# Float32r matmuls over 384 tokens instead of 288, in attention followed by two feed-forward layers

## The chip, the core and the metric

The kernel runs on one core of a Trainium2 chip. The metric is the device time of one launch in microseconds. The five engines of the core have queues of their own: TensorE multiplies (PE in the profile; its weight loads stand apart as PEld), VectorE (DVE), ScalarE (ACT) and GpSimd (POOL) work on elements, SyncE (SP) issues DMAs. In this kernel TensorE reads both operands from SBUF and accumulates in tiles of PSUM, in banks of 512 Float32 values per partition; VectorE and ScalarE empty them.

## The reference

Three steps follow one another, all in Float32 on the host side (B = 4, H = 8, S = 576, D = 64; 2304 tokens of 512 features between the steps):

```
a = softmax(causal(q k^T / 8));  local = a v
mem_out = (phi(q) M_prev) / (phi(q) z_prev + 1e-6)
x = sigmoid(beta) mem_out + (1 - sigmoid(beta)) local        # to 2304 x 512
x = (silu(x w_gate) * (x w_val)) w_out                       # d_ff 1536
y = (h * sigmoid(1.702 h)) w_out2,  h = x w_in               # d_ff 2048
```

## The kernel before, in words

**Numbers in two parts.** The two layers multiply in Float32r, one pass of the array per matmul. To keep accuracy each operand is split in a high and a low part, and each product is the sum of three: high by high, high by low, low by high. In `proj` (L618) these are `(0, xh), (0, xl), (1, xh)`, where 0 and 1 choose the weights' high or low part.

**Two passes over the tokens.** The first pass (`moe`, L616) does both layers for two of the four batches, 1152 tokens; the second (`second`, L784) does the other two. Weights are decoded and split once, during the first pass, in an order of 68 blocks of 128 x 512 (`next_w`, `ahead`, L187 to L196), and written to DRAM for the second, which reads them ready or half ready (`next_block`, `ready`, L746 to L759), eight blocks ahead.

**First pass.** For each group g (3 in the first layer, 4 in the second) four hidden blocks of 128 features are made and then multiplied back to 4 blocks of 128 outputs (d). The 1152 tokens are taken in two halves of 576. A half has a PSUM tile of two banks, [128, 2, 512], and each of the 12 products of a block is issued as two matmuls of 288 columns, one per bank, with a weight load each:

```
for s in range(2):
    mm(t[:, s, :NS], wp[:, w, c:c + 128], x[:, kd, h, s * NS:(s + 1) * NS],
       kd == 0 and i == 0, kd == 3 and i == 2)
```

So a half of a block is 24 matmuls, with TensorE passing through `mm` (L82). ScalarE and VectorE then empty the tile: tanh and one multiply-add for a gate (L642, L643), one multiply for a value (L652), and `split_h` (L609) makes the two parts `hh` and `hl` of the hidden value. `back` (L599) multiplies four hidden blocks with one block of output weights, again 24 matmuls per half, and the result is added to `acc` (L663, L665, L694, L696) or, at the end, goes to `ot` and out (L699 to L708). PSUM is shared in two pools: `ps_m` with two tiles for this and `ps_s` with two for the attention.

**Attention beside it.** The attention of the first two batches runs alone at the start, up to some 120 us. That of the other two is cut into steps, with estimated costs, and these steps are put between the yields of `moe` in proportion: each yield gives `HALF`, the time planned for half of the 24 matmuls, and steps are taken as long as their costs are below the share that `MOE_T` allows. Under these steps the tile framework plans the order of each engine's queue by a timeline of its own (`schedule_with_timeline_sim`); on the chip each queue runs in that order.

**Second pass.** The products of x with the layer's input weights use Strassen's seven block products (`unit`, L807; `prod`, L793), with 288 columns in two banks each, and the weights `wb`. The second products of each group call `back` for two halves of 576 as the first pass does (L873 to L898). All PSUM tiles here come from `big` in turn from `ps_s` and `ps_m`. The very last half is cut into two pieces of 288. `blocks_of_x` (L955) reads the second pass's x back and forms the seven blocks of X while the first pass ends.

Of the kernel before, what the change touches and what calls it, by code (L numbers as in the profile page):

```python
# [8 lines left out]
F32 = mybir.dt.float32  # L9
# [26 lines left out]
def tile_attention_moe_moe(  # L36
# [57 lines left out]
    HALF = 1.475  # L94
# [514 lines left out]
    def split_h(t):  # L609
        hh = hpool.tile([128, 2, NS], F32R, tag="hh", name="hh")  # L610
        hl = hpool.tile([128, 2, NS], F32R, tag="hl", name="hl")
        nc.scalar.copy(hh, t)  # L612
        nc.vector.tensor_sub(hl, t, f(hh))  # L613
        return hh, hl

    def moe(xh, xl):  # L616

        def proj(wp, t, h):  # L618
            for kd in range(4):
                c = kd * 128  # L620
                for i, (w, x) in enumerate(((0, xh), (0, xl), (1, xh))):
                    for s in range(2):
                        mm(t[:, s, :NS], wp[:, w, c:c + 128], x[:, kd, h, s * NS:(s + 1) * NS],
                           kd == 0 and i == 0, kd == 3 and i == 2)
                if kd == 1:
                    yield HALF

        def big():
            t = ps_m.tile([128, 2, 512], F32, tag="m", name="m")
            return t, t[:, :, :NS]  # L630

        acc = x1.tile([128, 4, 2, 2, NS], F32, tag="acc", name="acc")
        for g in range(3):
            hs = []
            for i in range(4):
                wp = next_w()
                us = []
                for h in range(2):
                    t, tg = big()
                    yield from proj(wp, t, h)  # L640
                    u = up.tile([128, 2, NS], F32, tag="u", name="u")
                    nc.scalar.activation(u, tg, AF.Tanh, scale=0.5)  # L642
                    nc.vector.scalar_tensor_tensor(u, u, 1.0, tg, op0=ALU.add, op1=ALU.mult)  # L643
                    us.append(u)
                    yield HALF
                wp = next_w()
                hs.append([])
                for h in range(2):
                    u = us[h]
                    t, tv = big()  # L650
                    yield from proj(wp, t, h)
                    nc.vector.scalar_tensor_tensor(u, u, 0.5, tv, op0=ALU.mult, op1=ALU.mult)  # L652
                    hs[i].append(split_h(u))
                    yield HALF
                flush()
            for d in range(4):
                wp = next_w()
                for h in range(2):
                    o, t = big()
                    yield from back(hs, wp, o, h)  # L660
                    ac = acc[:, d, h]
                    if g == 0:
                        nc.scalar.copy(ac, t)  # L663
                    else:
                        nc.vector.tensor_add(ac, ac, t)  # L665
                    if g == 2:
                        yh = xh[:, d, h].rearrange("p (s n) -> p s n", s=2)
                        yl = xl[:, d, h].rearrange("p (s n) -> p s n", s=2)
# [3 lines left out]
        acc = x1.tile([128, 4, 2, 2, NS], F32, tag="acc", name="acc2")  # L672
        for g in range(4):
            hs = []
            for i in range(4):
                wp = next_w()
                hs.append([])
                for h in range(2):
                    t, th = big()
                    yield from proj(wp, t, h)  # L680
                    u = up.tile([128, 2, NS], F32, tag="u", name="u")
                    nc.scalar.activation(u, th, AF.Tanh, scale=0.851)
                    nc.vector.scalar_tensor_tensor(u, u, 1.0, th, op0=ALU.add, op1=ALU.mult)  # L683
                    hs[i].append(split_h(u))
                    yield HALF
            for d in range(4):
                wp = next_w()
                for h in range(2):
                    t0 = h * S
                    o, t = big()  # L690
                    yield from back(hs, wp, o, h)
                    ac = acc[:, d, h]
                    if g == 0:
                        nc.scalar.activation(ac, t, AF.Copy, scale=0.5)  # L694
                    elif g < 3:
                        nc.vector.scalar_tensor_tensor(ac, t, 0.5, ac, op0=ALU.mult, op1=ALU.add)  # L696
                    else:
                        ot = up.tile([128, 2, NS], F32, tag="u", name="ot")
                        nc.vector.scalar_tensor_tensor(ot, t, 0.5, ac, op0=ALU.mult, op1=ALU.add)  # L699

                        def store(d=d, ot=ot, t0=t0):
                            nc.sync.dma_start(
                                out=out[d * 128:(d + 1) * 128, t0:t0 + S],
                                in_=ot.rearrange("p s n -> p (s n)"),
                            )
# [4 lines left out]

# [73 lines left out]
    def second(X):  # L784
        turn = [0]

        def big():
            turn[0] += 1
            if turn[0] % 2:
                return ps_s.tile([128, 2, 512], F32, tag="s", name="m")  # L790
            return ps_m.tile([128, 2, 512], F32, tag="m", name="m")
# [48 lines left out]
        def split(t, scale, eng):  # L840
            hh = hpool.tile([128, 2, NS], F32R, tag="hh", name="hh")
            hl = hpool.tile([128, 2, NS], F32R, tag="hl", name="hl")
# [5 lines left out]
            return hh, hl  # L848

        for layer, n in enumerate((3, 4)):  # L850
            acc = x1.tile([128, 4, 2, 2, NS], F32, tag="acc", name="acc")
            for g in range(n):
                hs = [[None, None] for k in range(4)]
                if layer == 0:
                    for k in range(4):
                        gates = {}

                        def done(row, h, c):
                            if row == 0:
                                gates[h] = gate(c, 0.5)  # L860
                            else:
                                nc.gpsimd.tensor_mul(c, c, gates[h])
                                hs[k][h] = split(c, 0.5, nc.vector)

                        unit(done)
                else:
                    for k in (0, 2):

                        def done(row, h, c):
                            hs[k + row][h] = split(gate(c, 0.851), 1.0, nc.gpsimd if row else nc.vector)  # L870

                        unit(done)
                for d in range(4):  # L873
                    wp = next_block()
                    for h in range(2):
                        tail = layer == 1 and g == n - 1 and d == 3 and h == 1
                        for sub in ((0,), (1,)) if tail else ((0, 1),):
                            o = big()
                            for _ in back(hs, wp, o, h, sub):
                                pass  # L880
                            ac = acc[:, d, h, sub[0]:sub[-1] + 1]
                            t = o[:, sub[0]:sub[-1] + 1, :NS]
                            if layer == 0:
                                if g == 0:
                                    nc.scalar.copy(ac, t)
                                else:
                                    nc.vector.tensor_add(ac, ac, t)
                            elif g == 0:
                                nc.scalar.activation(ac, t, AF.Copy, scale=0.5)
                            elif g < n - 1:  # L890
                                nc.vector.scalar_tensor_tensor(ac, t, 0.5, ac, op0=ALU.mult, op1=ALU.add)
                            else:
                                ot = cu.tile([128, len(sub), NS], F32, tag="sn", name="ot")
                                nc.vector.scalar_tensor_tensor(ot, t, 0.5, ac, op0=ALU.mult, op1=ALU.add)
                                c0 = (2 + h) * S + sub[0] * NS
                                nc.sync.dma_start(
                                    out=out[d * 128:(d + 1) * 128, c0:c0 + len(sub) * NS],
                                    in_=ot.rearrange("p s n -> p (s n)"))  # L898
            if layer == 0:
                halves(lambda k, h: acc[:, k, h].rearrange("p s n -> p (s n)"), X)  # L900

    MOE_T = NCK * 4 * HALF
# [85 lines left out]
    flush()  # L988
    second(X)
# [42 lines left out]
```

## Time and profile before

| | |
|---|---|
| median of 3 runs | 1081.12 us (1080.79 to 1081.13) |
| span of the profiled execution | 1080.3 us |
| lying around the span, against the median | 0.8 us |
| TensorE matmul, weight load busy | 1041.8 us (96%), 971.8 us (90%) |
| VectorE, ScalarE, GpSimd busy | 696.1 us (64%), 542.9 us (50%), 612.3 us (57%) |
| TensorE matmuls in the trace | 7664 |
| DMA | 133.93 MB, mean 124 GB/s |

The profiler notes the start and the end of each instruction. Matmuls are pipelined: one is noted as busy until its result is in PSUM, so a busy TensorE can still be slower than it might be, and the distance from start to start is read where rows merge several matmuls ("x4"). The granted clock (PEclk) is TensorE's share of 2.4 GHz; 0.50 is 1.2 GHz.

### The profile page before, as it was taken

The numbers are of one execution on the slowest core, as the hardware profiler recorded it, in microseconds if no ns is written. First come the engines' busy times: TensorE is split into PE (matmuls) and PEld (weight loads), VectorE is DVE, ScalarE is ACT, GpSimd is POOL, SyncE is SP. The second block draws the span as 40 slices with busy tenths as digits, with TensorE's granted clock in tenths as the row PEclk, the third lists the DMA queues.
The fourth block names the chain that finished last, engine by engine and source line by source line (L and its number), as shares of the span: only waits on it lengthen the run. The fifth ranks groups of instructions, "written<-read, shape, count | busy, mean of one in ns | idle before, by whom it ended". The sixth has DMA issues, their size and how long they took to land.

```text
span 1080.3 us, 19843 instructions
## 1 busy us (share of the span) xinstructions
PE 1041.8 (96%) x7664; PEld 971.8 (90%) x7664; DVE 696.1 (64%) x1063; ACT 542.9 (50%) x1107; POOL 612.3 (57%) x634
## 2 busy tenths in 40 slices
PE   5989798999999999999999999999999999999998
PEld 2656687899999898989899999999999999999998
DVE  6887589646666777836657448762745778265573
ACT  4887555655545555756556454442513436343230
POOL 6886798866567475665745542661835817153321
PEclk8999999999999999999999999999999999999999
DMA  4332635644454453444434337323222222322102
GB/s 165 114 95 87 216 118 187 219 148 146 151 170 142 132 174 123 157 137 147 161 122 140 115 127 278 110 71 110 70 79 87 85 78 70 112 74 74 59 21 88
DMA packets 46718, 133.93 MB, mean 124 GB/s; under 512 B 7584, under 2 KB 10400, under 8 KB 46624
## 3 DMA queue, kind: packets, MB, share of 16 engines
q1 hardware_dynamic: 46480, 132.67, 36.7%
q8 instruction: 60, 0.98, 0.4%
q14 instruction: 34, 0.28, 0.1%
q10 hardware_dynamic: 144, 0.00, 0.0%
HBM read 92.54 MB, written 40.11 MB: 123 GB/s over the span
## 4 chain that ended last, share of the span: by engine, by line
PE 54%; DVE 3%; ACT 1%; DMA 1%; POOL 1%; issue 1%; SPq 0%; ACTq 0%; DVEq 0%; POOLq 0%
PE m L82 51%; PE o L82 1%; PE s L82 1%; DVE hl L613 1%; PE tp L378 1%; DMA xr<-x 0%; DMA raw<-w 0%; DVE u L683 0%; ACT hh L612 0%; ACT wb L742 0%; POOL wa L150 0%; DVE xl L766 0%; DMA x<-st 0%; DVE wa L147 0%; POOL p L366 0%
## 5 line engine op out<-in xcount | busy, mean ns | idle before, releaser
L82 PE MATMUL m<-hh,wp 128*128 128x288 f32 x1792 | 312.6, 297 | 1.4 <-ACT acc L663 0.7
L82 PEld LDWEIGHTS m<-hh,wp 128*128 128x128 f32 x1792 | 262.2, 189 | 9.5 <-issue 3.2
L82 PE MATMUL m<-xh,wp 128*128 128x288 f32 x1280 | 241.8, 304 | 12.6 <-DVE u L643 8.9
L743 POOL TENSOR_TENSOR wb<-raw,wb 128x256 fp32r<-128x256 f32 x140 | 124.9, 906 | 197.4 <-ACT wb L742 192.3
L82 PEld LDWEIGHTS m<-xh,wp 128*128 128x128 f32 x1280 | 193.9, 191 | 23.8 <-DVE u L643 8.1
L82 PE MATMUL m<-hl,wp 128*128 128x288 f32 x896 | 190.6, 296 | 0.0
L150 POOL TENSOR_TENSOR wa<-wa,wr 128x512 uint32<-128x512 uint32 x68 | 93.6, 1377 | 106.3 <-issue 50.2
L82 PEld LDWEIGHTS m<-hl,wp 128*128 128x128 f32 x896 | 143.6, 188 | 0.4 <-issue 0.4
L82 PE MATMUL m<-xl,wp 128*128 128x288 f32 x640 | 138.2, 298 | 0.0
L82 PE MATMUL m<-xh,wb 128*128 128x288 f32 x640 | 119.0, 296 | 0.0
L169 POOL TENSOR_TENSOR wp<-wa,wp 128x512 fp32r<-128x512 f32 x68 | 92.7, 1364 | 42.5 <-ACT wp L166 42.1
L82 PEld LDWEIGHTS m<-xl,wp 128*128 128x128 f32 x640 | 104.4, 191 | 0.0
L82 PEld LDWEIGHTS m<-xh,wb 128*128 128x128 f32 x640 | 96.9, 189 | 0.0
L742 ACT CAST wb<-raw 128x256 fp32r<-128x256 f32 x140 | 55.6, 404 | 79.1 <-PE m L82 77.6
L366 POOL TENSOR_SCALAR p<-p,sm 128x128 f32<-128x128 f32 (+3 forms) x128 | 75.1, 605 | 28.6 <-DVE sm L357 8.5
L82 PE MATMUL m<-th,wb 128*128 128x288 f32 x480 | 90.3, 296 | 0.0
L144 DVE TENSOR_SCALAR wa<-wa 128x512 f32<-128x512 f32 x68 | 39.3, 578 | 75.6 <-ACT wa L140 75.0
L341 ACT ACTIVATE p<-s,nm 128x128 f32<-128x128 f32 (+3 forms) x128 | 66.0, 528 | 30.5 <-DVE nm L327 29.3
L82 PEld LDWEIGHTS m<-th,wb 128*128 128x128 f32 x480 | 73.2, 189 | 0.0
L140 ACT ACTIVATE wa<-w 128x512 f32<-128x512 f32 x68 | 46.0, 677 | 53.5 <-POOL wp L169 48.9
L613 DVE TENSOR_TENSOR hl<-u,hh 128x576 fp32r<-128x576 f32 x56 | 56.4, 1007 | 25.4 <-ACT hh L612 24.6
L141 ACT ACTIVATE wr<-w 128x512 uint32<-128x512 uint16 x68 | 46.1, 678 | 51.0 <-POOL wa L150 50.4
(136 smaller groups left out, 1830.6 us busy)
## 6 DMA issues: line engine op xcount, KB each, us to landing
w<-w SPq DMA_DIRECT2D x40, 512.0 KB, 3.7
raw<-w SPq DMA_DIRECT2D x20, 896.0 KB, 4.6
w<-wo SPq DMA_DIRECT2D x28, 512.0 KB, 3.6
w<-wp SPq DMA_DIRECT2D x28, 512.0 KB, 2.9
wp<-w SPq DMA_DIRECT2D x28, 512.0 KB, 3.5
w<-sums SPq DMA_DIRECT2D x20, 512.0 KB, 2.8
qk<-qk SPq DMA_DIRECT2D x32, 288.0 KB, 3.7
nq<-nat SPq DMA_DIRECT2D x16, 320.0 KB, 4.1
```

The lines of the kernel that those rows point to most:

```text
L82: nc.tensor.matmul(o, w, x, start=start, stop=stop)
L140: nc.scalar.activation(a, top.bitcast(F32), AF.Abs)
L141: nc.scalar.activation(r, rest, AF.Copy, scale=2.0 ** -13)
L144: nc.vector.tensor_scalar(a, a, HIGH, LOW, op0=ALU.min, op1=ALU.max)
L150: nc.gpsimd.tensor_tensor(au, au, r, op=ALU.add)
L169: nc.gpsimd.tensor_sub(wp[:, 1], t, f(wp[:, 0]))
L341: nc.scalar.activation(p[:, j, c:c + n], s[:, j, c:c + n], AF.Exp, bias=nm[:, x, j:j + 1], accum_out=sm[:, x, j:j + 1])
L366: nc.gpsimd.tensor_scalar(p[:, j, c:c + n], p[:, j, c:c + n], sm[:, x, j:j + 1], 1.0, op0=ALU.mult, op1=ALU.mult)
L378: nc.tensor.transpose(t[:, j, c:c + 128], p[:, j, c:c + 128], ident)
L613: nc.vector.tensor_sub(hl, t, f(hh))
L742: nc.scalar.copy(wb[:, 0], src)
L743: nc.gpsimd.tensor_sub(wb[:, 1], src, f(wb[:, 0]))
```

## The change

All Float32r matmuls of the first pass, and the second products of the second pass, take three pieces of 384 tokens instead of two halves of two times 288. A piece has a PSUM tile of one bank, and each of its 12 products is one matmul:

```
-    HALF = 1.475
+    NT = 384
+    HALF = 0.983
...
-    def back(hs, wp, t, h, sub=range(2)):
+    def back(hs, wp, o, c):
         for k in range(4):
-            hh, hl = hs[k][h]
+            hh, hl = hs[k]
             for i, (w, x) in enumerate(((0, hh), (1, hh), (0, hl))):
-                for s in sub:
-                    mm(t[:, s, :NS], wp[:, w, k * 128:(k + 1) * 128], x[:, s, :],
-                       k == 0 and i == 0, k == 3 and i == 2)
+                mm(o, wp[:, w, k * 128:(k + 1) * 128], x[:, c:c + NT], k == 0 and i == 0, k == 3 and i == 2)
...
+    def split_new():
+        return [hpool.tile([128, 2 * S], F32R, tag=n, name=n) for n in ("hh", "hl")]
+
+    def split_h(hs, u, c):
+        hh, hl = (x[:, c:c + NT] for x in hs)
+        nc.scalar.copy(hh, u)
+        nc.vector.tensor_sub(hl, u, f(hh))
...
+        def bank():
+            return ps_m.tile([128, 512], F32, tag="m", name="m")[:, :NT]
...
+                for c in COLS:
+                    t = bank()
+                    yield from proj(wp, t, c)
+                    u = new_u()
+                    nc.scalar.activation(u, t, AF.Tanh, scale=0.5)
+                    nc.vector.scalar_tensor_tensor(u, u, 1.0, t, op0=ALU.add, op1=ALU.mult)
+                    us.append(u)
+                    yield HALF
```

The hidden parts of one block lie in one tile of 1152 tokens (4 slots) instead of two of 576 (8 slots). Everything that empties a tile works on 384 columns, three times instead of twice. Stores of the output are three per block. The pools and the seam between the passes:

```
-    ps_m = ctx.enter_context(
-        tc.tile_pool(name="ps_m", bufs=2, space=bass.MemoryType.PSUM, reuse_waits="tile"))
-    ps_s = ctx.enter_context(
+    pstack = ExitStack()
+    ps_m = pstack.enter_context(
+        tc.tile_pool(name="ps_m", bufs=4, space=bass.MemoryType.PSUM, reuse_waits="tile"))
+    ps_s = pstack.enter_context(
         tc.tile_pool(name="ps_s", bufs=2, space=bass.MemoryType.PSUM, reuse_waits="tile"))
-    up = ctx.enter_context(tc.tile_pool(name="up", bufs=3))
-    hpool = ctx.enter_context(tc.tile_pool(name="hpool", bufs=8))
+    up = ctx.enter_context(tc.tile_pool(name="up", bufs=4))
+    hpool = ctx.enter_context(tc.tile_pool(name="hpool", bufs=4))
...
     flush()
+    pstack.close()
+    ps_c = ctx.enter_context(
+        tc.tile_pool(name="ps_c", bufs=4, space=bass.MemoryType.PSUM, reuse_waits="tile"))
     second(X)
```

In the second pass the products of X keep their two banks and 288 columns, now from four tiles of `ps_c`; the second products use one bank of such a tile, for all pieces, and the cut of the very last half goes:

```
-                    for h in range(2):
-                        tail = layer == 1 and g == n - 1 and d == 3 and h == 1
-                        for sub in ((0,), (1,)) if tail else ((0, 1),):
-                            o = big()
-                            for _ in back(hs, wp, o, h, sub):
-                                pass
+                    for c in range(0, 2 * S, NT):
+                        o = big()[:, 0, :NT]
+                        for _ in back(hs, wp, o, c):
+                            pass
```

The splits of the second pass still write halves of 576, into the new tiles of 1152. `MOE_T` becomes `NCK * 6 * HALF`, 401.1 planned units instead of 401.2.

## Rows read from the trace of the kernel before

**Rows 1.** Windows by stage: stretch and length, busy us and count per engine, clock, DMA

```profile
119.60:200.00 80.40, 68.50 (x464) 63.96 (x463) 63.61 (x90) 42.92 (x86) 68.22 (x65) 0.94 0.60 193
200.00:645.00 445.00, 442.71 (x3282) 411.58 (x3281) 277.57 (x446) 245.74 (x476) 268.81 (x265) 1.00 0.43 146
```

**Rows 2.** Windows of the instructions that use wp: TensorE, loads, ScalarE, GpSimd

```profile
119.60:200.00 80.40, 60.66 (x406) 58.42 (x407) 6.17 (x10) 13.51 (x10) 0.94 0.60 193
200.00:645.00 445.00, 374.14 (x2650) 355.12 (x2649) 33.88 (x55) 73.98 (x55) 1.00 0.43 146
645.00:1080.30 435.30, 209.03 (x1557) 207.50 (x1555) 0.61 (x1) 3.12 (x2) 1.00 0.27 91
```

**Rows 3.** Chain of waits, its last long link: start, us, engine, line, count

```profile
666.22 410.87 PE m L82 x3082
```

**Rows 4.** Waits of TensorE, 119 to 200 us, then 200 to 645: total, times, longest

```profile
PE m L82 <- DVE u L643: 8.9, 4, 4.2
PE m L82 <- DVE u L652: 2.4, 2, 1.4
...
PE m L82 <- DVE acc L665: 1.3, 1, 1.3
```

**Rows 5.** Timeline of TensorE at low clock (start, us), and that stretch's window

```profile
133.87 1.16 PE L82 MATMUL m<-xh,wp 128*128 128x288 f32 x4
134.83 0.68 PE L82 MATMUL m<-xl,wp 128*128 128x288 f32 x2
...
133.20:138.10 4.90, 4.90 (x22) 4.90 (x22) 4.61 (x6) 3.24 (x5) 4.62 (x7) 0.50 0.53 208
```

**Rows 6.** Timeline of TensorE, Float32 matmuls of the attention: first alone, then all four

```profile
421.82 0.40 PE L82 MATMUL o<-ph,mz 128*128 128x288 f32 x1
...
421.82 1.13 PE L82 MATMUL o<-ph,mz 128*128 128x288 f32 x4
```

**Rows 7.** Groups of weight loads by shape: busy us, mean ns, idle before

```profile
L82 PEld LDWEIGHTS m<-hh,wp 128*128 128x128 f32 x1792 | 262.2, 189 | 9.5 <-issue 3.2 <-ACT acc L663 1.6 <-ACT acc L694 1.1
...
L82 PEld LDWEIGHTS o<-pt,v 128*64 128x64 f32 x448 | 29.3, 137 | 8.8
...
L82 PEld LDWEIGHTS o<-ph,mz 128*128 128x128 f32 x64 | 11.4, 194 | 4.5 <-ACT pz L401 1.8 <-ACT p L341 0.6
```

**Rows 8.** Timeline of VectorE at the end: 576 columns, then 288

```profile
1073.94 0.76 DVE L894 SCALAR_TENSOR_TENSOR ot<-m,acc 128x576 f32<-128x576 f32 x1 [2.44 <-PE m L82]
...
1077.12 0.46 DVE L894 SCALAR_TENSOR_TENSOR ot<-m,acc 128x288 f32<-128x288 f32 x1 [1.14 <-PE m L82]
```

**Rows 9.** Groups of ScalarE by shape: casts of 256 and of 512 columns

```profile
L742 ACT CAST wb<-raw 128x256 fp32r<-128x256 f32 x140 | 55.6, 404 | 79.1 <-PE m L82 77.6 <-POOL wb L743 0.6
...
L166 ACT CAST wp<-wa 128x512 fp32r<-128x512 f32 x68 | 41.8, 616 | 20.5 <-PE m L82 19.0 <-POOL wa L150 1.4
```

**Rows 10.** Timeline at the seam of the passes, TensorE and VectorE

```profile
660.38 0.43 PE L82 MATMUL m<-xh,wb 128*128 128x288 f32 x2
...
666.22 0.40 PE L82 MATMUL m<-hh,wp 128*128 128x288 f32 x1 [0.55 <-DVE ot L699]
...
674.09 1.43 DVE L766 TENSOR_TENSOR tl<-xr,th 128x576 fp32r<-128x576 f32 x2
...
678.04 0.42 PE L82 MATMUL m<-hl,wp 128*128 128x288 f32 x2
```

**Rows 11.** Timeline where a group's second products begin, second pass, first layer

```profile
718.83 0.69 PE L82 MATMUL m<-hh,wp 128*128 128x288 f32 x4
...
724.18 0.76 DVE L845 SCALAR_TENSOR_TENSOR hl<-sn,hh 128x576 fp32r<-128x576 f32 x1 [2.03 <-ACT hh L843]
...
725.28 0.64 ACT L885 COPY acc<-m 128x576 f32<-128x576 f32 x1 [1.14 <-PE m L82]
```

**Rows 12.** Timeline where the first pass's second layer begins, TensorE and ScalarE

```profile
419.59 0.53 PE L82 MATMUL m<-xh,wp 128*128 128x288 f32 x2 [1.33 <-DVE acc L665]
...
421.94 0.69 ACT L669 CAST xh<-acc 128x576 fp32r<-128x576 f32 x1
```

More of the change, by code (lines that the diff above doesn't have):

```diff
@@ L621, in proj, with new_u @@
                 for i, (w, x) in enumerate(((0, xh), (0, xl), (1, xh))):
-                    for s in range(2):
-                        mm(t[:, s, :NS], wp[:, w, c:c + 128], x[:, kd, h, s * NS:(s + 1) * NS],
-                           kd == 0 and i == 0, kd == 3 and i == 2)
+                    mm(t, wp[:, w, c:c + 128], x[:, kd, c0:c0 + NT], kd == 0 and i == 0, kd == 3 and i == 2)
                 if kd == 1:
                     yield HALF
[L628 to L632, printed above, removed]
+        def new_u(name="u"):
+            return up.tile([128, NT], F32, tag="u", name=name)
+        COLS = range(0, 2 * S, NT)
+        acc = flat(x1.tile([128, 4, 2, S], F32, tag="acc", name="acc"))
         for g in range(3):
@@ L646, in moe @@
                 wp = next_w()
[L647 to L653, printed above, removed]
+                hs.append(split_new())
+                for c, u in zip(COLS, us):
+                    t = bank()
+                    yield from proj(wp, t, c)
+                    nc.vector.scalar_tensor_tensor(u, u, 0.5, t, op0=ALU.mult, op1=ALU.mult)
+                    split_h(hs[i], u, c)
                     yield HALF
@@ L657, in moe @@
                 wp = next_w()
[L658 to L661, printed above, removed]
+                for c in COLS:
+                    o = bank()
+                    yield from back(hs, wp, o, c)
+                    ac = acc[:, d, c:c + NT]
                     if g == 0:
-                        nc.scalar.copy(ac, t)
+                        nc.scalar.copy(ac, o)
                     else:
-                        nc.vector.tensor_add(ac, ac, t)
+                        nc.vector.tensor_add(ac, ac, o)
                     if g == 2:
-                        yh = xh[:, d, h].rearrange("p (s n) -> p s n", s=2)
-                        yl = xl[:, d, h].rearrange("p (s n) -> p s n", s=2)
+                        yh, yl = (x[:, d, c:c + NT] for x in (xh, xl))
                         nc.scalar.copy(yh, ac)
@@ L676, in moe @@
                 wp = next_w()
[L677 to L684, printed above, removed]
+                hs.append(split_new())
+                for c in COLS:
+                    t = bank()
+                    yield from proj(wp, t, c)
+                    u = new_u()
+                    nc.scalar.activation(u, t, AF.Tanh, scale=0.851)
+                    nc.vector.scalar_tensor_tensor(u, u, 1.0, t, op0=ALU.add, op1=ALU.mult)
+                    split_h(hs[i], u, c)
                     yield HALF
@@ L687, in moe, with store @@
                 wp = next_w()
[L688 to L692, printed above, removed]
+                for c in COLS:
+                    o = bank()
+                    yield from back(hs, wp, o, c)
+                    ac = acc[:, d, c:c + NT]
                     if g == 0:
-                        nc.scalar.activation(ac, t, AF.Copy, scale=0.5)
+                        nc.scalar.activation(ac, o, AF.Copy, scale=0.5)
                     elif g < 3:
-                        nc.vector.scalar_tensor_tensor(ac, t, 0.5, ac, op0=ALU.mult, op1=ALU.add)
+                        nc.vector.scalar_tensor_tensor(ac, o, 0.5, ac, op0=ALU.mult, op1=ALU.add)
                     else:
[L698 to L705, printed above, removed]
+                        ot = new_u("ot")
+                        nc.vector.scalar_tensor_tensor(ot, o, 0.5, ac, op0=ALU.mult, op1=ALU.add)
+                        def store(d=d, ot=ot, c=c):
+                            nc.sync.dma_start(out=out[d * 128:(d + 1) * 128, c:c + NT], in_=ot)
                         flush()
@@ L838, in gate, with split @@
             return t
-        def split(t, scale, eng):
-            hh = hpool.tile([128, 2, NS], F32R, tag="hh", name="hh")
-            hl = hpool.tile([128, 2, NS], F32R, tag="hl", name="hl")
+        def split(hs, h, t, scale, eng):
+            hh, hl = (x[:, h * S:(h + 1) * S] for x in hs)
+            t = t.rearrange("p s n -> p (s n)")
             nc.scalar.activation(hh, t, AF.Copy, scale=scale)
@@ L847, in split @@
                 eng.tensor_sub(hl, t, f(hh))
-            return hh, hl
         for layer, n in enumerate((3, 4)):
-            acc = x1.tile([128, 4, 2, 2, NS], F32, tag="acc", name="acc")
+            acc = x1.tile([128, 4, 2, S], F32, tag="acc", name="acc")
+            af = acc.rearrange("p k h s -> p k (h s)")
             for g in range(n):
-                hs = [[None, None] for k in range(4)]
+                hs = [split_new() for k in range(4)]
                 if layer == 0:
@@ L869, in done @@
                         def done(row, h, c):
-                            hs[k + row][h] = split(gate(c, 0.851), 1.0, nc.gpsimd if row else nc.vector)
+                            split(hs[k + row], h, gate(c, 0.851), 1.0, nc.gpsimd if row else nc.vector)
                         unit(done)
@@ new lines, in second @@
+                    for c in range(0, 2 * S, NT):
+                        o = big()[:, 0, :NT]
+                        for _ in back(hs, wp, o, c):
+                            pass
+                        ac = af[:, d, c:c + NT]
+                        if layer == 0:
+                            if g == 0:
+                                nc.scalar.copy(ac, o)
+                            else:
+                                nc.vector.tensor_add(ac, ac, o)
+                        elif g == 0:
+                            nc.scalar.activation(ac, o, AF.Copy, scale=0.5)
+                        elif g < n - 1:
+                            nc.vector.scalar_tensor_tensor(ac, o, 0.5, ac, op0=ALU.mult, op1=ALU.add)
+                        else:
+                            ot = cu.tile([128, NT], F32, tag="sn", name="ot")
+                            nc.vector.scalar_tensor_tensor(ot, o, 0.5, ac, op0=ALU.mult, op1=ALU.add)
+                            nc.sync.dma_start(out=out[d * 128:(d + 1) * 128, 2 * S + c:2 * S + c + NT], in_=ot)
```

48 lines of the change are left out of this document (9 added, 39 removed).

## The prediction, made before the changed kernel ran

> **What bounds the kernel now.** I read four views, in this order. First the windows by stage: from 200 us on, TensorE is busy all the time (442.7 of 445 us up to 645 us) while VectorE, ScalarE and GpSimd are each at 55 to 62% [rows 1]; before 200 us it is busy in 68.5 of 80.4 us, and GpSimd in 68.2. Second the chain of waits: its last link but one is a single run of 3082 matmuls in 410.87 us, which nothing interrupts [rows 3]. So from the seam between the passes to the end the time is matmul count times the distance from one matmul's start to the next, (410.87 - 0.30) / 3081 = 133.3 ns. Third the waits of TensorE: 8.9 + 2.4 us before 200 us, all on VectorE emptying a PSUM tile, and 1.3 us on it in the 445 us after [rows 4]. Fourth the matmul itself, since a tenth of its 133.3 ns isn't explained by its columns: 288 columns at 2.4 GHz are 120.0 ns.
>
> **What the 13.3 ns are.** Three readings decide the forecast. (a) In the stretch in which the granted clock is 0.50 (1.2 GHz), four matmuls start in 134.83 - 133.87 = 0.96 us, 240 ns each: exactly 288 columns at 1.2 GHz, and nothing on top [rows 5]. (b) Plain Float32 matmuls of the attention, at full clock, also with 288 columns and a weight load each, run at (1.13 - 0.40) / 3 = 0.243 us per record [rows 6], 3 ns above 240; each takes two cycles a column. (c) Their weight loads and those of the Float32r matmuls last alike, 194 and 189 ns, and a load of 64 columns lasts 137 [rows 7]: 52 ns for 64 columns, so the streaming part of a 128-column load is about 104 ns and the rest a lead. All three fit one reading: a load starts when the matmul ahead starts, needs some 130 ns before the next may start, and is hidden wherever the matmul streams longer than that. At 120 ns it isn't hidden, and the load is the floor. Then 384 columns (160 ns at 2.4 GHz) hide it, and the matmul costs 160 plus the 3 ns of (b): 163 ns. Bounds for this operation, which the trace doesn't show: below, 160 (no surcharge, as in (a)); above, 177.7, the same 0.463 ns per column as now. A fixed surcharge of 13.3 would give 173.3. I take 163, since (b) has the same weights, load and clock.
>
> The Trainium skill, "TensorE: Matmul & The Clock Gate", section on the back-to-back issue gap, gives N/2.4 + 2.5 ns for a matmul by itself. By it four of 288 cost 490 ns and three of 384 cost 487.5: the change would be worth 2.5 ns per four, 1152 x 2.5 = 2.9 us in all, an estimate from that page. The row says 133.3 and not 122.5 [rows 3], so the rule misses what this stream of load and matmul pairs costs today. The same page (Part 3, the mechanism) says that a weight load overlaps a running matmul only in another row group; here every load takes all rows, and 133.3 ns is less than 104 + 120, so they do overlap to a large part. If a part stays uncovered whatever the length, that is the first rival.
>
> **The change, part by part.**
> 1. Matmuls. The first pass has 68 weight blocks x 2 halves x 24 = 3264 matmuls of 288 columns, the second products 28 x 48 = 1344; both counts are in the rows that use wp (406 + 2650 + 1557, five of them cut by an edge) [rows 2]. They become 2448 and 1008 of 384. The 1680 of the products with wb stay. Per four old ones: 533.2 - 3 x 163 = 44.2 ns, 1152 times: 50.9 us. By place: 406 / 4 x 44.2 = 4.5 us before 200 us; 2650 / 4 x 44.2 = 29.3 us up to 645 us; 208 / 4 x 44.2 = 2.3 us in the rest of the first pass; 336 x 44.2 = 14.9 us in the second. The last two lie in the run without a stop and count in full.
> 2. Before 200 us TensorE isn't the bound all the time, GpSimd is at 85%. I count half of the 4.5 us, so 2.2 are lost. Ends: none of it gained, or more than it, since four one-bank tiles let TensorE run 3 x 12 x 163 ns = 5.9 us ahead of a late VectorE instead of one tile of 24 x 133 = 3.2 us, and the 11.3 us of waits there could shrink by up to 8.
> 3. More, shorter instructions on VectorE and ScalarE: three of 384 for two of 576. VectorE takes 0.76 us for 576 and 0.46 for 288 [rows 8], so 0.16 fixed; 92 more instructions in the first pass (24 blocks with one or two, 16 with two, 20 accumulations, 4 splits of the layer's end) are 15 us. ScalarE takes 616 ns for 512 and 404 for 256 [rows 9], so 0.19 fixed, and 68 more are 13 us. Between 200 and 645 us, which becomes some 416 us, VectorE goes to (277.6 + 13) / 416 = 70% and ScalarE to 63%. TensorE covers that; if a queue is late now and then it costs. I take 1.5 us, and for the deeper tiles 1.3 us back, the waits of rows 4 after 200 us. Ends: -2 to +8.
> 4. The seam. Now the second pass's products start at 660 us between the first pass's last ones; TensorE's one stop there is 0.55 us, and the last Float32r block of X is written until 675.5 us, 2.9 us before the first pass's last matmul ends [rows 10]. The new pool lies on the banks of the old two, so I assume that no product starts before the last tile of the first pass is emptied: 0.76 us of VectorE [rows 8] and the hand-overs around it, about 1.5 us less the 0.5 of today, +1.0. Behind that matmul only TensorE's own queue waits, with wb blocks made ahead. The first pass's last products need 144 x 163 = 23.5 us instead of 25.6, and without the early products between them they end before X is complete; but the seven products read X in the order in which it is written, 1.6 us apart, so X isn't late for more than a us or so. Ends: 0 to +4, the upper with a store queue that holds an output tile back (four slots of 12 matmuls, 7.8 us, instead of three of 24, 9.6 us).
> 5. Second products read hidden values that come late: they start at 718.83, the last half is split at 724.94, the first tile is emptied at 725.28, and TensorE fills the gap with the k = 0 to 2 parts of four open tiles [rows 11]: 4 x 18 x 133.3 = 9.6 us of filling for 6.1. Afterwards 4 x 9 x 163 = 5.9 us. That is short by 0.2 us if every piece waits for the last half; pieces of the first 384 columns need the first half only, if regions of a tile are followed one by one, as they are for x (TensorE reads it at 419.59, ScalarE writes another slice of it at 421.94 [rows 12]). Seven groups: +1.0, ends 0 to +5.
> 6. The end: the last two matmul groups of 288 become one of 384, emptied in 0.16 + 0.4 = 0.56 us against 0.46, and a third more to store: +0.2.
> The hidden tiles (same bytes, half the slots) and weight blocks cost nothing: a slot's last reader stands in TensorE's queue ahead of anything whose result is written there, and eight blocks are prepared ahead.
>
> Sum: 50.9 - 2.2 - 1.5 + 1.3 - 1.0 - 1.0 - 0.2 = 46.3 us. The profiled span is 1080.3 us, the median of the runs 1081.1, so 0.8 lie around it. 1081.1 - 46.3 = 1034.8 us.
>
> **The rivals.**
> - Fixed surcharge: part of each load stays uncovered, 13.3 ns at any width. For it: that load and matmul share the array. Against: (a) and (b), where nothing of the load shows. Time: 533.2 - 3 x 173.3 = 13.3 ns x 1152 = 15.3 us, less 0.7 (half of what falls before 200 us) and the 2.2 of parts 4 to 6: 1069.
> - The first pass doesn't follow: the chains through VectorE, ScalarE and GpSimd (decode, split, softmax) set its length as before 200 us, and only 2.3 + 14.9 us come. For it: waits shorter than TensorE's queue don't show. Against: 55 to 62% busy after 200 us. Time: 1081.1 - 17.2 + 2.2 = 1066.
> - Slower: the moving operand's columns are the limit at full clock, 0.463 ns each. It decides from 177.7 ns per matmul, where three cost what four do; every ns above costs 3.5 us. Then nothing is gained and the costs remain: 2.2 us of parts 4 to 6 (1083), with part 3's 8 us of late queues 1091; I give 1087. For it: no other one-cycle width in the trace. Against: the Float32 passes read the same bytes in twice the time, which doesn't exclude it; the uneven surcharge between the clocks speaks for a floor.
>
> **How the numbers follow.** Load as floor 0.81, fixed surcharge 0.07, first pass bound elsewhere 0.06, column rate 0.06. The first has a range of its own from 1022 (161 ns a matmul, 3 x 2 ns x 1152 = 6.9 us less, and 6 us of the early waits gone) to 1050 (the upper ends of parts 3, 4 and 5 together). For 8 in 10 I leave out the lower tail beyond 1022 and most of the rivals, and go a little above 1050 for the first pass following in part: 1022 to 1056. What a measurement here can tell from no change is about 0.2%, 2 us. The first three cases are faster, 0.94, less 0.02 for their upper tails; the column rate is 0.04 slower and 0.02 within. So faster 0.92, within it 0.03, slower 0.05.
>
> **What would show it.** In the new profile: the distance between 384-column matmuls in the last 400 us (163 right; 173 or 178 the rivals); 2448 + 1008 matmuls of 384 columns beside the 1680 of 288; TensorE's waits before 200 us (some 11 us or less); a stop of 1 to 2 us at the seam; gaps at the start of each group of second products. I am wrong if the distance is above 170 ns, or if it is 163 and TensorE stands idle for more than 10 us after 200 us.

## The result, and the profile after

The changed kernel takes 1072.9 us (median of 4, 1069.1 to 1073.5) against 1081.1 before: ratio 0.991, interval 0.989 to 0.993. It is faster by 8.2 us; 1034.8 was forecast, with 1022 to 1056 as the range. The profiled execution is 1071.0 us long, 9.3 less than before.

Windows of the changed kernel, columns as in [rows 1]; the third is the stretch of the seam:

```profile
119.60:200.00 80.40, 72.67 (x395) 66.50 (x392) 63.41 (x96) 44.23 (x91) 67.41 (x64) 0.96 0.64 211
200.00:645.00 445.00, 443.94 (x2678) 408.45 (x2677) 284.57 (x537) 253.32 (x545) 273.18 (x273) 1.00 0.44 150
645.00:700.00 55.00, 50.02 (x338) 49.41 (x337) 41.81 (x60) 24.03 (x47) 23.09 (x25) 0.94 0.44 154
```

TensorE is at least as busy as before up to 645 us; at the seam it is busy in 50.0 of 55 us, at a granted clock of 0.94. The timeline of TensorE in the second pass (start, us) shows the distance that the forecast hung on:

```profile
799.67 0.51 PE L82 MATMUL m<-hh,wp 128*128 128x384 f32 x2
...
800.19 0.51 PE L82 MATMUL m<-hh,wp 128*128 128x384 f32 x2
...
801.75 0.51 PE L82 MATMUL m<-hh,wp 128*128 128x384 f32 x2
```

Twelve matmuls start in 801.75 - 799.67 = 2.08 us: 173.3 ns each, not 163. That is 160 ns for the columns at 2.4 GHz and the same 13.3 on top as 288 columns have over 120 [rows 3].

TensorE's waits from 119 to 640 us (total, times, longest), to be set beside [rows 4]:

```profile
PE m L82 <- DVE u L649: 5.8, 5, 1.9
PE tp L379 <- ACT p L342: 1.9, 1, 1.9
PE m L82 <- DVE hl L614: 0.9, 1, 0.9
```

The seam, to be set beside [rows 10]: TensorE, then VectorE, then the window that follows:

```profile
660.20 0.34 PE L82 MATMUL m<-hl,wp 128*128 128x384 f32 x1
664.49 0.82 PE L82 MATMUL m<-xh,wb 128*128 128x288 f32 x2 [3.95 <-issue]
...
663.16 0.76 DVE L777 TENSOR_TENSOR xr<-xr,t 128x576 f32<-128x576 f32 x1
663.83 0.56 DVE L702 SCALAR_TENSOR_TENSOR ot<-m,acc 128x384 f32<-128x384 f32 x1
...
664.40:669.40 5.00, 4.91 (x20) 4.94 (x21) 2.00 (x3) 1.17 (x3) 0.58 (x1) 0.50 0.19 70
```

The first pass's last matmul starts at 660.20 us, but VectorE empties its tile only at 663.83, because work on the blocks of X (L771, L773, L762, L777) and two earlier emptyings stand ahead in its queue, and the first product of the second pass starts 0.1 us after that ends. After this stop (4.3 us from start to start, 3.95 of them idle) the granted clock is 0.50, 1.2 GHz, for 5 us: 20 matmuls at 240 instead of 133 ns, 2.1 us more. The chain of waits after it, to be set beside [rows 3, 11]:

```profile
664.49 225.25 PE m L82 x1548
...
903.54 1.61 DVE hl L839
905.20 1.52 PE m L82 x7
906.75 0.50 ACT acc L878
907.29 47.15 PE m L82 x309
954.47 0.57 DVE acc L880
```

Before, one run of 3082 matmuls reached the end; now it breaks where groups begin, for late hidden values (`hl`) and for tiles still to be emptied (`acc`). Added over all gaps above a matmul's own distance, these stops are 2.7 us after 672 us, and were under 0.1.

**Where the time went, by stage.** The first pass from its first matmul (119.69 us before, 120.88 after) to its last (678.17, 660.20), with the products of the second pass that ran inside it (early products: 5.6 us before, none after) counted to the second: 552.9 before, 539.3 after, 13.6 us less. The second, to its last matmul: 404.2 and 407.1, 2.8 us more.

### The profile page after: what moved, and what is told of

It reads as the page before. It is cut to its first block, busy times and chain, and to the rows that moved or that the text cites. A ratio compares the mean times of both kernels' runs of the same rounds, so it can differ in the third digit from the quotient of the medians.

```text
span 1071.0 us, 17769 instructions
## 1 busy us (share of the span) xinstructions
PE 1031.8 (96%) x6512; PEld 953.1 (89%) x6512; DVE 695.8 (65%) x1174; ACT 549.7 (51%) x1183; POOL 605.3 (57%) x634
## 4 chain that ended last, share of the span: by engine, by line
PE 53%; DVE 3%; POOL 2%; issue 2%; ACT 1%; DMA 0%; SPq 0%; POOLq 0%; DVEq 0%
PE m L82 49%; PE o L82 1%; PE s L82 1%; POOL wb L739 1%; PE tp L379 1%; DVE hl L614 1%; DMA xr<-x 0%; POOL wp L170 0%; POOL wa L151 0%; DVE u L687 0%; SPq L953 0%; DVE u L829 0%; DVE xl L762 0%; DVE wa L148 0%; ACT u L828 0%
## 5 line engine op out<-in xcount | busy, mean ns | idle before, releaser
L82 PE MATMUL m<-hh,wp 128*128 128x384 f32 x1344 | 343.2, 338 | 1.5 <-DVE ot L702 1.0
L82 PE MATMUL m<-xh,wp 128*128 128x384 f32 x960 | 260.0, 343 | 5.8 <-DVE u L649 5.8
L82 PEld LDWEIGHTS m<-hh,wp 128*128 128x128 f32 x1344 | 240.7, 188 | 12.2 <-issue 5.9
L739 POOL TENSOR_TENSOR wb<-raw,wb 128x256 fp32r<-128x256 f32 x140 | 122.4, 888 | 198.4 <-ACT wb L738 192.6
L82 PE MATMUL m<-hl,wp 128*128 128x384 f32 x672 | 222.7, 337 | 1.4 <-DVE hl L614 0.9
L82 PEld LDWEIGHTS m<-xh,wp 128*128 128x128 f32 x960 | 175.4, 189 | 16.1 <-DVE u L649 8.2
L82 PE MATMUL m<-xl,wp 128*128 128x384 f32 x480 | 161.5, 337 | 0.0
L82 PEld LDWEIGHTS m<-hl,wp 128*128 128x128 f32 x672 | 126.2, 188 | 4.5 <-DVE hl L614 2.1
L82 PEld LDWEIGHTS m<-xl,wp 128*128 128x128 f32 x480 | 90.7, 189 | 0.9 <-issue 0.4
L614 DVE TENSOR_TENSOR hl<-u,hh 128x384 fp32r<-128x384 f32 x84 | 63.0, 754 | 30.2 <-ACT hh L613 29.5
```

The lines of the kernel that those rows point to most:

```text
L82: nc.tensor.matmul(o, w, x, start=start, stop=stop)
L614: nc.vector.tensor_sub(hl, u, f(hh))
L739: nc.gpsimd.tensor_sub(wb[:, 1], src, f(wb[:, 0]))
```

## The experiments

All times are medians; the kernel before took 1081.2 to 1081.7 beside them. Short names: `after` is the changed kernel. Edits are shown in part; "..." marks what is left out.

**Matmuls alone.** Kinds of matmul in a row, 48 each, in two alternating banks:

```diff
+REP = 48
...
+    WIDTHS = (512, 448, 384, 320, 288, 256, 192, 128, 64)
...
+    def run(x, w, n, parts=128):
+        for i in range(REP):
+            nc.tensor.matmul(ps[0:parts, i % 2, 0:n], w, x, start=True, stop=True)
...
+    for n in WIDTHS:
+        run(rs[n], wr, n)
```

These are Float32r (`rs`, `wr`). Then come weights of 64 columns (`wh`), bfloat16 (`wb`) and Float32 (`wf`).

> Matmuls alone, 48 of each kind in a row with a weight load each, and none of the reference's computation. Read: the distance from start to start within each kind, after a warm-up of 48 matmuls of 512 columns. Theory S (a Float32r matmul costs its columns at 2.4 GHz and 13.3 ns on top, whatever its weight load): 512 columns 226.7 ns, 448 200, 384 173.3, 320 146.7, 288 133.3, 256 120, 192 93.3, then a floor by the weight load; with weights of 64 columns the same 173.3 and 133.3; bfloat16 with a load each 162 and 122 for 384 and 288. Theory L (the 13.3 ns are a part of the weight load that no matmul covers): the same for full weights, but about half of it, 167 and 127 ns, with weights of 64 columns, and the 13.3 stay with bfloat16 if its load lasts as long. The forecast's theory, a floor of some 130 ns: 384 columns 163 ns; the profile of the changed kernel already speaks against it.

Groups by shape (count, busy us, mean ns of one, idle before), with the bfloat16 loads last; a distance from start to start is about (busy - mean) / 47:

```profile
L47 PE MATMUL ps<-r,wr 128*128 128x512 f32 x48 | 11.1, 389 | 0.0
...
L47 PE MATMUL ps<-r,wr 128*128 128x384 f32 x48 | 8.5, 334 | 0.0
L47 PE MATMUL ps<-b,wb 128*128 128x384 bf16 x48 | 8.0, 326 | 0.0
...
L47 PE MATMUL ps<-r,wr 128*128 128x288 f32 x48 | 6.5, 294 | 0.0
L47 PE MATMUL ps<-h,wh 128*64 128x288 f32 x48 | 6.5, 293 | 0.0
L47 PE MATMUL ps<-b,wb 128*128 128x288 bf16 x48 | 6.0, 286 | 0.0
...
L47 PE MATMUL ps<-r,wr 128*128 128x192 f32 x48 | 5.5, 274 | 0.0
L47 PE MATMUL ps<-r,wr 128*128 128x128 f32 x48 | 5.5, 274 | 0.0
L47 PE MATMUL ps<-h,wh 128*64 128x128 f32 x48 | 3.0, 222 | 0.0
...
L47 PEld LDWEIGHTS <-wb 128*128 128x128 bf16 x144 | 12.1, 98 | 4.3
```

From the starts themselves: 227.1 ns for 512 columns, 202.7 for 448, 173.4 for 384, 131.8 for 288, 118.6 for 256, then 111.2 for 192 and 111.0 for 128. So there is a floor by the weight load, but it is 111 ns, and 288 columns lie above it. From 256 columns up each Float32r matmul costs its columns and 12 to 16 ns, within 3 ns of what theory S says. With weights of 64 columns, whose load is 54 ns shorter (median 134 against 188), 288 columns take 131.1, no less; theory L wanted 127. Matmuls of 128 columns then take 60, so the shorter load moves the floor. That is 6.5 ns above their 53.3 and not 13.3, so below 256 columns the surcharge isn't the same, and these runs don't say how it goes there. (The last matmuls of 64 columns, and the first of 384 with 64-column weights right behind them, ran at a granted clock of 0.50; the last 30 of the latter take 175.0 ns.)

bfloat16 with a load each takes 162.7 and 122.5: 2.5 to 2.7 ns on top; but its load lasts 98 ns, so it says nothing on theory L. Theory S holds from 256 columns up, theory L falls by the shorter load.

At 128 columns the load (some 104 ns of streaming, by the forecast's estimate) and the matmul (53) share 111 ns, so some 46 ns of them overlap: such a load runs beside a matmul over the same rows, against the sentence of the Trainium skill that the forecast weighed ("TensorE: Matmul & The Clock Gate", Part 3, the mechanism).

The Trainium skill's 2.5 ns per matmul ("TensorE: Matmul & The Clock Gate", back-to-back issue gap) is thus what bfloat16 shows here (162.7 and 122.5 ns); Float32r pays some five times that (173.4 and 131.8).

**Parts of the array.** The same with other kinds, all Float32r:

```diff
+        run(rows[0:64, :n], wr[0:64], n)
...
+        run(cols[:, :n], wq, n, 32)
...
+        run(pair.rearrange("p (a n) -> p a n", a=2)[:, :, :n // 2], wr, n)
...
+        run((swap[:, :n], swop[:, :n]), (wr, ws), n)
...
+        one(tail[:, :n], wr, n)
```

That is 64 rows; weights of 32 columns; the moving operand in two runs; two weights and two operands in turn; one bank and one accumulation.

> Matmuls alone, Float32r, 48 of a kind with 384 and then 288 columns, and none of the reference's computation. Kinds: as before (173.4 and 131.8 ns); 64 rows of the array instead of 128; weights of 32 columns; the moving operand as two runs; two weights and two moving tiles in turn; all into one bank as one accumulation. If the surcharge of 12 to 13 ns belongs to the moving operand's stream at full rate, all kinds show it. If it is a change of weights in the array, 64 rows or 32 columns make it smaller. If it is the accumulation or the bank, only the last kind differs.

Groups by shape, columns as above:

```profile
L52 PE MATMUL ps<-rows,wr 64*128 64x384 f32 x48 | 8.6, 333 | 0.0
L56 PE MATMUL ps<-tail,wr 128*128 128x384 f32 x48 | 8.5, 335 | 0.0
L52 PE MATMUL ps<-cols,wq 128*32 128x384 f32 x48 | 8.5, 336 | 0.0
...
L52 PE MATMUL ps<-full,wr 128*128 128x384 f32 x48 | 8.5, 334 | 0.0
```

All kinds take 173.4 to 176.7 ns, and 131.1 to 133.2 with 288 columns. The surcharge follows neither the weights, the rows nor the bank. That it belongs to the moving operand's stream of 4-byte values at a column per cycle is what is left of the causes named above; no run shows it by itself.

**The structure without the width.** Four pieces of 288 in place of three of 384 in `after`:

```diff
-    NT = 384
-    HALF = 0.983
+    NT = 288
+    HALF = 0.7375
```

(and six slots for `u`, `MOE_T` with 8 pieces)

> The changed kernel with four pieces of 288 tokens, each with a one-bank tile of its own (output-tile pool of 6 slots instead of 4): the change's structure without its width. Surcharge theory: 1152 x (533.2 - 3 x 173.7) = 13.9 us more than the changed kernel from the matmuls, and some more from 128 more instructions on VectorE and ScalarE: 1086 to 1090 us, slower than before the change. Rival, the gain comes from the one-bank tiles and not from the width: 1073 us or less.

1083.6 us, below the range expected; ratio to before 1.0018 (1.0007 to 1.0029), 10.7 more than `after`. So the width is worth 10.7 us, less than the 13.9 of its matmuls, and the change without it is a loss of some 2 us, about the least that can be told from none.

**The seam, twice.** First without a new pool: products of x from `ps_s`, second products from `ps_m`.

```diff
-            return ps_c.tile([128, 2, 512], F32, tag="c", name="m")
+            return ps_s.tile([128, 2, 512], F32, tag="s", name="m")
+
+        def bank():
+            return ps_m.tile([128, 512], F32, tag="m", name="m")[:, :NT]
...
-                        o = big()[:, 0, :NT]
+                        o = bank()
```

> The changed kernel without the new pool at the seam: the second pass's products of x take their tiles from ps_s (two of two banks), its second products from ps_m (four of one bank). If the pool is what holds the second pass's first product back until the first pass's last output tile is emptied (that emptying stands in VectorE's queue behind the blocks of X): the stop of 4.3 us at the seam and the low clock after it go, 6 to 7 us: about 1066 us. Rival: X itself is late, so the first product can't start sooner: the stop stays and the time is 1072 to 1074. Two slots for the products of x may cost a few us in the second pass; then the seam in the trace decides, not the time.

1081.6 us; a miss in time. The first product of the second pass starts at 654.5, 5.3 us before the first pass's last matmul, so X isn't late. But with two tiles for the products the second pass pays it back. TensorE's timeline at the seam, then its waits from 655 us on:

```profile
654.48 0.42 PE L82 MATMUL m<-xh,wb 128*128 128x288 f32 x2
...
PE m L82 <- ACT hh L838: 4.2, 3, 2.1
PE m L82 <- DVE sn L809: 3.0, 2, 2.0
```

Then with the same four tiles as in `after`, but only `ps_m`'s banks in the new pool:

```diff
+            turn[0] += 1
+            if turn[0] % 4 in (1, 2):
+                return ps_s.tile([128, 2, 512], F32, tag="s", name="m")
             return ps_c.tile([128, 2, 512], F32, tag="c", name="m")
...
-        tc.tile_pool(name="ps_c", bufs=4, space=bass.MemoryType.PSUM, reuse_waits="tile"))
+        tc.tile_pool(name="ps_c", bufs=2, space=bass.MemoryType.PSUM, reuse_waits="tile"))
```

(`ps_s` is opened ahead of `ps_m` and stays open)

> The changed kernel with ps_s kept through the second pass and only the banks of ps_m opened anew (two tiles of two banks); the first two products of the second pass use ps_s. If the pool is the cause of the stop at the seam: no stop longer than 1 us, the clock stays at 1.00 there, about 1066 us, with four two-bank tiles as in the changed kernel. If X is late: 1072 to 1074 us.

1067.2 us, ratio 0.986 (0.985 to 0.988): 5.7 less than `after`, and the fastest version. Its window of the seam:

```profile
645.00:700.00 55.00, 54.42 (x382) 54.09 (x381) 45.98 (x64) 27.71 (x55) 29.82 (x29) 1.00 0.48 168
```

The stop of 4.3 us is gone (the longest one left there has 0.6 us of idle time, behind ScalarE's `sn`), the granted clock is 1.00, and 44 more matmuls fit in. The first product starts at 655.8, again 5.3 us before the first pass's last matmul. With as many tiles and X made the same way, the new pool over all eight banks is the cause. Call this kernel `kept`; the runs that follow are changes to it, but for the one in the old pools, which is `after` with the pools of before.

**The width, pass by pass.** Pieces of 288 in the second products of the second pass only, then in the first pass only, then in both:

```diff
-                    for c in range(0, 2 * S, NT):
-                        o = big()[:, 0, :NT]
+                    for c in range(0, 2 * S, NS):
+                        o = big()[:, 0, :NS]
```

(and `NS` for `NT` in what follows; the first pass as in the four pieces above)

> As the run with ps_s kept (1067.2 us), with the second pass's second products in four pieces of 288 again. Surcharge theory: 336 x (4 x 133.2 - 3 x 173.7) = 3.9 us more, 1071 us, and a little more for 28 more emptyings: 1070 to 1073. Rival, in the second pass the width brings nothing or loses: 1065 to 1068.

> As the run with ps_s kept (1067.2 us), with the first pass in four pieces of 288 (one bank each), the second pass's second products in three of 384. Surcharge theory: 816 x (4 x 133.2 - 3 x 174.0) = 8.8 us more, 1076 us, with more and shorter instructions 1075 to 1079. Rival, the first pass is set by the other engines, so that TensorE's width does nothing there: 1067 to 1069.

> As the run with ps_s kept (1067.2 us), with four pieces of 288 in both passes: the change's structure without its width and without its seam. If the parts add up (second pass +5.0, first pass +3.0 in the runs with one of them): 1075 us. With the surcharge alone, 1152 x 11.7 ns = 13.5 us: 1081 us. Against the kernel before it tells what the structure is worth by itself: 6 us faster in the first case, nothing in the second.

1072.2, 1070.2 and 1077.8 us: 5.0, 3.1 and 10.7 more than `kept`. In the second pass the width is worth what its matmuls say (336 x 11.7 ns = 3.9) and a us more, in the first 3 of 9.5 (816 x 11.7 ns): neither rival as written, nearer to the one that lets the other engines set the first pass. The two don't add up to what both together cost, 2.6 us more. And `kept` without its width is 3.9 us faster than before (0.997, 0.996 to 0.998), between the two cases that were named. The us more in the second pass is in the waits from 655 us on, of the run with 288 there and then of `kept`:

```profile
PE m L82 <- DVE hl L844: 1.9, 3, 0.8
PE m L82 <- DVE sn L822: 0.6, 1, 0.6
PE m L82 <- ACT sn L808: 0.4, 1, 0.4
```

```profile
PE m L82 <- ACT sn L808: 0.6, 1, 0.6
PE m L82 <- DVE hl L844: 0.5, 1, 0.5
```

Four open pieces of 288 hold less work than four of 384 to fill the wait for the last hidden values with, which is the mechanism of part 5 of the forecast.

**The width in the old pools.** Two pieces in the two banks of one tile, pools and seam as in the kernel before (a change to `after`):

```diff
+        two = []
+
         def bank():
-            return ps_m.tile([128, 512], F32, tag="m", name="m")[:, :NT]
+            if not two:
+                t = ps_m.tile([128, 2, 512], F32, tag="m", name="m")
+                two.extend((t[:, 0, :NT], t[:, 1, :NT]))
+            return two.pop(0)
```

> The width alone: three pieces of 384 as in the changed kernel, but in the PSUM pools of the kernel before (two pieces share a two-bank tile of ps_m in the first pass; the second pass takes its tiles in turn from ps_s and ps_m) and no new pool at the seam. Surcharge theory and no harm from the pairs: 12 to 15 us less than before from the matmuls, 2 to 3 back for more instructions: 1068 to 1071 us, with no stop of 4 us at the seam. If the one-bank tiles of their own are what shortened TensorE's waits in the first pass (8.2 us of DVE u and acc waits less than before): those waits come back and the time is 1073 us or more.

1119.0 us, 38 slower than before. TensorE's waits from 119 to 690 us:

```profile
PE m L82 <- DVE u L692: 20.3, 14, 2.6
PE m L82 <- DVE u L654: 10.9, 7, 3.0
```

A pair is given back when both pieces are emptied, and with three pieces to a block every other pair spans two blocks. The planned order changed with it: the attention's last matmul is at 515.6 us, not at 621.9 as in `kept`. The run doesn't separate the two.

**Fewer tiles, and pairs in the second pass.**

```diff
-        tc.tile_pool(name="ps_m", bufs=4, space=bass.MemoryType.PSUM, reuse_waits="tile"))
+        tc.tile_pool(name="ps_m", bufs=3, space=bass.MemoryType.PSUM, reuse_waits="tile"))
```

> As the run with ps_s kept (1067.2 us), with three one-bank tiles for the first pass's pieces instead of four: 1152 columns in flight, as many as the two tiles of 576 of the kernel before. If the 8 us that the first pass gains without any width (four pieces of 288 against two tiles of 576) come from the larger number of columns in flight, they are lost again: 1073 to 1077 us. If they come from the finer grain (a tile is given back after 12 matmuls and one emptying), most stay: 1067 to 1070 us.

1073.1 us, 5.9 lost, 5.0 of them in the first pass (542.5 against 537.5 us by stage, early products taken out). That is some two fifths of the 12.2 us that the structure brings there (below); it goes when 1152 columns are in flight in place of 1536, as many as before the change, and the rest stays. TensorE's waits from 119 to 640 us, then two of `kept`:

```profile
PE m L82 <- DVE u L649: 5.8, 4, 2.4
PE m L82 <- DVE acc L670: 1.8, 2, 1.6
PE m L82 <- DVE u L657: 1.5, 2, 1.1
PE m L82 <- ACT acc L668: 1.4, 1, 1.4
...
PE m L82 <- DVE u L649: 4.6, 5, 1.8
PE m L82 <- DVE acc L670: 0.6, 1, 0.6
```

The waits for tiles to be emptied are 10.5 us, 5.2 in `kept`; but all waits together are only 1 us more. The order differs too: TensorE goes over from products to the attention 100 times in the first pass, 84 times in `kept`. What the columns in flight do by the waits and what by the order isn't separated.

And pairs for the second products of `kept`:

```diff
-                        o = big()[:, 0, :NT]
+                        if not two:
+                            o = big()
+                            two.extend((o[:, 0, :NT], o[:, 1, :NT]))
+                        o = two.pop(0)
```

> As the run with ps_s kept (1067.2 us), with two second products of the second pass in the two banks of one tile, so that eight pieces may be open instead of four. If the stops at the start of the groups (2.7 us in all) come from too few open pieces while the last hidden values are late, they go: 1064 to 1066 us. Rival: a pair is given back only when both pieces are emptied, and the plan of the queue gets worse, as with the pairs in the first pass: 1068 us or more.

1071.9 us, 4.8 more than `kept`: the rival. Stops of 0.2 to 0.6 us at the start of the groups remain, and in the last group TensorE waits for tiles, as the chain's end shows:

```profile
1056.98 2.37 PE m L82 x12
1059.54 0.31 issue
1059.85 0.56 DVE ot L892
```

## Why the prediction was wrong, step by step

**Step 1, the matmuls, is the one that failed.** It says that a load "needs some 130 ns before the next may start, and is hidden wherever the matmul streams longer than that". The load's floor is 111 ns, and 133.3 was never that floor but 120 plus a surcharge of Float32r. With 173.3 in place of 163 the term is (533.2 - 519.9) x 1152 = 15.3 us instead of 50.9; the runs give 10.7. The reading of the rows was possible in two ways, a maximum and a sum, and all Float32r rows had one width, where both agree. The three readings that were to decide didn't: (a) at 1.2 GHz and (b) with two cycles a column are both streams at half rate, in which the surcharge isn't seen; (c) shows how long a load lasts, not when it is covered. The first rival had the right cost per matmul, though not for its reason, a part of the load left uncovered; it was given 0.07. That its time, 1069, is nearly right is luck in part: it counts none of the 12.2 us that the structure brings in the first pass, nor the 5.9 and 6.3 us lost in the second pass and by the new pool, and these cancel; and it has nearly all of the width's 15.3 us come through.

**Steps 2 and 3, the first pass.** By stage (first pass, with early products taken out), four pieces of 288 in `kept`'s structure take 540.7 us against 552.9: the structure alone brings 12.2, where 2.2 were taken off and 8 named as the outer end. Up to 4 of the 12.2 us are TensorE's clock: that it falls stood in [rows 1, 5], and the forecast put it at nothing. Before, the clock is granted at 0.50 for 10.2 us in all, in or right after the two longest waits for a tile, 4.2 [rows 4] and 2.07 us. The second of these and the two windows before, then the window and the longest wait with four pieces of 288 (the run with 288 in both passes):

```profile
169.15 0.78 PE L82 MATMUL m<-xh,wp 128*128 128x288 f32 x2 [2.07 <-DVE u L643]
131.60:138.40 6.80, 5.65 (x23) 5.66 (x24) 6.17 (x7) 4.71 (x8) 6.52 (x8) 0.50 0.63 244
169.20:172.60 3.40, 3.40 (x14) 3.40 (x15) 3.37 (x6) 3.40 (x9) 2.67 (x4) 0.50 0.26 96
...
119.60:200.00 80.40, 72.77 (x510) 66.50 (x507) 63.17 (x108) 45.04 (x101) 67.30 (x63) 1.00 0.64 215
PE m L82 <- DVE u L649: 4.5, 5, 1.7
```

Some 37 products at 240 instead of 133 ns are 3.9 us. With four pieces of 288 the waits are shorter, and the clock stays at 1.00; in `after` it is at 0.50 for 6.8 us up to 200 us, right behind two waits of 1.9 us.

The width adds 3.2 (537.5 in `kept`), where 36.1 were forecast up to the seam and 9.5 would follow from 816 x 11.7 ns. Two other runs with the same first pass (288 in the second pass, pairs in the second pass) have 536.3 and 535.6, so that the width's part is 3.2 to 5.1 us. That more and shorter instructions bring VectorE and ScalarE to their limits isn't seen: with pieces of 384 they are busy 284.6 and 253.3 of 445 us. The missing 4 to 6 us lie for the most part where TensorE changes between products and attention: these changes hold 24.2 to 24.6 us above a product's own distance in the three runs with 384, 20.1 with 288. The planned order differs between the two kernels too; no run separates why.

**Step 4, the seam.** +1.0 was taken, with +4 as the end; 5.7 us measured between `after` and `kept` (6.3 by stage). The mechanism was named, products waiting for the last tile to be emptied, but it was priced as one emptying. What stands ahead of that emptying in VectorE's queue, the making of X, and the low clock after the stop weren't counted.

**Step 5, the groups' starts.** +1.0 taken, 2.7 measured, the mechanism as told. **Step 6**, the end: from the last matmul's start to the end of the span 3.7 us against 3.5, +0.2 as forecast.

The sum by stage, against the profile of before: structure of the first pass -12.2, its width -3.2, width in the second -7.5 (6.0 by the run with 288 there alone), structure in the second +5.9, new pool +6.3, a later start of the first pass +1.2, the end +0.2; together -9.3 us, as between the two spans. The second's -7.5 and +5.9 hold the stops at the groups' starts, 6.2 us with pieces of 288 and 2.7 with 384. Each stage is read from one profile of each kernel, and the first pass starts between 119.2 and 122.1 us in all of them, behind the same attention code; so a difference of 1 or 2 us here isn't sure, and the +1.2 may be nothing but that.

## What to carry to other kernels

A distance between matmuls that exceeds its columns may be a floor or a surcharge; where all rows have one width, the trace can't tell which, and a gain that rests on the floor deserves a short run of matmuls alone, with other widths. Count PSUM in columns in flight and in the unit that is given back: four tiles of one bank beat three by 5.9 us, and pairs of pieces in one tile, with the order that was planned for them, made the first pass some 49 us longer (586.8 against 537.5, early products taken out). When a pool is opened anew over banks in use, price the wait with everything that stands ahead of the last reader in its engine's queue, and leave banks that are idle out of it.

## What the runs showed that had not been expected

At 2.4 GHz and from 256 columns up, Float32r costs 12 to 16 ns per matmul above its columns (384 columns: 173.4), bfloat16 2.5 to 2.7 (162.7), Float32 3 (243.1 for 288 columns at two cycles each); at 1.2 GHz Float32r shows none [rows 5]. A Float32r weight load of 128 columns sets a floor of 111 ns, one of 64 columns no more than 60. A stop of 4.3 us was followed by 5 us at half clock, a third of the seam's price. And in the run of matmuls alone the granted clock was 0.50 from 85.2 to 92.0 us although TensorE had been busy without a gap, with matmuls of 128 and then 64 columns; why isn't shown.
